# Hand-written orders for the last chunk, inverses earlier, a V split later, bias constants behind a mark

## The chip, the cores and the metric

One core of a Trainium2 chip runs the whole program. The metric is the device time of one execution in microseconds (us); the median of three runs of the kernel before is 841.37 us.

## The reference, cut to what matters

Sliding-window attention, a dense gated layer, and a routed layer of eight experts, one behind the other, all in float32 (`moe_w_*` arrive as float64 and are converted on the chip):

```python
scores = where(mask, q @ k.T / sqrt(64) + slope * -|i - j|, -1e9)     # 4 x 8 heads, 576 x 576, window 128
attn = softmax(scores) @ v
x = attn.transpose(0, 2, 1, 3).reshape(2304, 512)
x = ((x @ w_a) * (x @ w_b)) @ w_out                    # d_ff = 1536
logits = x @ w_gate + modality_bias[modality_id]       # 8 experts
e = argmax(logits); gate = softmax(logits)[e]
out[token] = gate * (relu(x @ w1[e]) @ w2[e])          # F = 1024
```

## The kernel before

The 2304 tokens are cut into seven chunks of 3, 2, 2, 3, 3, 3 and 2 tiles of 128 (`CH`, L34). A chunk goes through the dense layer in twelve steps `j`, one for each 128 columns of `d_ff`: `mm_ab` (L485) makes `x @ w_a` and `x @ w_b` in two PSUM banks (`psa`, `psb`), ScalarE copies the first out (`asb`), VectorE multiplies (`gf`), and one step later `mm_out` (L501) adds the product times `w_out` into PSUM. From chunk 1 on, `gf` is split into a rounded part (ScalarE cast) and a rest (VectorE subtraction), since matmuls run on pairs of reduced-precision values.

**Attention runs inside the steps of the chunk ahead.** One item is one 128-row tile of a pair of heads. An item takes three steps: in the first its scores are computed (`score_mm`), reduced on VectorE (`score_red`) and exponentiated on ScalarE; in the second VectorE inverts the sum (`score_invs`, two small instructions), ScalarE scales by it (`score_nrm`, L295), TensorE transposes (`pt_tr`, L304), ScalarE and VectorE copy and split (`pt_cp`, L317 and L318), and GpSimd masks it into `pt` (L320, L322); in the third TensorE multiplies by V (`a_pv`, L370) and ScalarE copies out (`pv_out`, L379). V has a split of its own (`prep_va` on ScalarE, `prep_vd` on VectorE) out of `vr`, which has a single buffer, so the next pair's load waits for it.

**Chunk 0** is special twice. Its own attention runs ahead of everything, items 0 to 11, in the first 42 us (the head). Its twelve steps (`step0`) then also convert the float64 weights on VectorE: for each step three instructions on 128x1024 words (`f64_ops`, tile `f64f`), the subtraction `rest` (L444) behind ScalarE's cast (`hi`, L441), and three on 128x512 words for `w_out` (`f64o`). I call this VectorE's list of a step: `step0` takes turns between `da` (`rest` and the three `f64f`) and `db` (the three `f64o`, then the inverses). `mm_out` of the step before waits for the third `f64o`; `late_rests` and `gf` stand behind the whole list.

**Orders.** In `step0` and `step` (chunks 1 to 5) the order on TensorE, ScalarE and VectorE is the order of the code (`tc.manual_schedule`); a planner orders SyncE's DMA queue and GpSimd, and, in chunk 6, all engines. Each engine runs its queue in order. In chunk 6 (two tiles, 256 columns) there is no attention left; it carries the routing of chunks 4 and 5: 24 dot products (`rd_dot`, L593, three for each expert, whose gate row `wgt` comes by DMA into one of two halves), then `route_fin` for three tiles, the choice of the expert that starts first (`early`), the gather of its tokens, the split of its `w1` (L877) and the transposes of its tokens (`u_xT`). The expert layers follow (L1190, L1207): `gen0` is the first.

`consts_b` builds the table of modality biases on GpSimd in six instructions (L755 to L765) from a small load `mid_i`. The code calls it in step 2 of chunk 0; the planner is free to put it earlier.

Of the kernel before, what the change touches and what calls it, by code (L numbers as in the profile page):

```python
# [7 lines left out]
F32 = mybir.dt.float32  # L8
F32R = mybir.dt.float32r
# [5 lines left out]
ALU = mybir.AluOpType  # L15
# [6 lines left out]
def attn_moe_moe2(ctx: ExitStack, tc, q, k, v, moe_w_a, moe_w_b, moe_w_out, modality_id,  # L22
# [18 lines left out]
    RD = (2, 3, 4, 5)  # L41
    PCB = 1
    LDA = 6
    EJ = 1
    SAT = 3
    PRP = 1
    HPS = 2000
# [611 lines left out]
    def new_preps(gk, gv):  # L659
        d = stage["d"]  # L660
        for a in stage["k"]:
            for h in range(2):
                prep_qa(a, h)
                d.append(lambda a=a, h=h: prep_qd(a, h))
        stage["q"] += stage["k"]
        stage["k"] = []
        while pos["prep"] < len(plist) and first[plist[pos["prep"]]] < gk:
            a = pairs[plist[pos["prep"]]]
            if a.c in S32:
                a_prep_q(a)  # L670
                prep_va(a)
                d.append(lambda a=a: prep_vd(a))
                pos["prep"] += 1
                continue
            prep_ka(a)
            d.append(lambda a=a: prep_kd(a))
            stage["k"].append(a)
            pos["prep"] += 1
        while stage["q"] and first[stage["q"][0].c, stage["q"][0].hp] < gv:
            a = stage["q"].pop(0)  # L680
            prep_va(a)
            d.append(lambda a=a: prep_vd(a))
# [191 lines left out]
    def split(dst, srcw, early=False):  # L874
# [4 lines left out]
        for k in range(srcw.shape[1]):  # L879
            nc.scalar.copy(out=dst[:, 0, k], in_=srcw[:, k])  # L880
            (nc.gpsimd if k < W2P else nc.vector).tensor_tensor(out=dst[:, 1, k], in0=srcw[:, k], in1=dst[:, 0, k], op=ALU.subtract)

    def u_w1(ev, pool):
        W1 = []
        for f in range(4):
            r = pool.tile([P, KD, 2 * P], F32, tag="wr", name="wr1")
            nc.sync.dma_start(out=r.rearrange("p k f -> p (k f)"),
                              in_=w1[bass.ds(ev, 1), f].rearrange("o p x -> p (o x)"))
            t = w1p.tile([P, 2, KD, 2 * P], F32R, tag="w1", name="w1s")
            split(t, r)  # L890
            W1.append(t)
        return W1

    def u_w2(ev, pool, early=False):
        W2 = []
# [22 lines left out]
        with tc.high_priority(offset=HPXT):  # L918
            return u_xT_(xg, nt, pool, bank)

    def u_xT_(xg, nt, pool, bank):
        xT = pool.tile([P, 2, KD, UT], F32R, tag="xT", name="xT")
        for kk in range(KD):
            ps = bank("ps_t")
            for t in range(nt):
                nc.tensor.transpose(ps[:, t * P:(t + 1) * P], xg[:, t, kk * P:(kk + 1) * P], ident)
            nc.scalar.copy(out=xT[:, 0, kk, :nt * P], in_=ps[:, :nt * P])
            nc.vector.tensor_tensor(out=xT[:, 1, kk, :nt * P], in0=ps[:, :nt * P], in1=xT[:, 0, kk, :nt * P],
                                    op=ALU.subtract)
        return xT  # L930
# [34 lines left out]
    def step0(j, pend, sc, tp):  # L965

        n, last = CH[0] * P, j == NJ - 1
        new = list(range(cur["s"], goal[j]))
        its = [live[g] for g in tp] if j else []
        if j + 2 < NJ:  # L970
            job[j + 2] = wab_jobs(j + 2)
        js = job.get(j + 2, [])

        da = [job.pop(j + 1)[4]] if j + 1 in job else []
        da += js[:3 if j else 2]
        db = [f for i in ((j - 1, j) if last else (j - 1,)) if i >= 0 for f in wo_jobs(i)]
        for g in sc:
            db += score_invs(live[g])
        while da or db:
            for d in (da, db):  # L980
                if d:
                    d.pop(0)()
        psa = mm_ab(0, j, 0, None if j else 1)
        asb = m1.tile([P, MT * P], F32, tag="asb", bufs=1, name="asb")
        nc.scalar.copy(out=asb[:, :n], in_=psa[:, :n])
        for g in sc:
            score_nrm(live[g])
        late_rests()
        psb = mm_ab(0, j, 1)
        gf = m1.tile([P, MT * P], F32, tag="g", bufs=2, name="gf")  # L990
        nc.vector.tensor_tensor(out=gf[:, :n], in0=psb[:, :n], in1=asb[:, :n], op=ALU.mult)
        for f in () if j else js[2:3]:
            f()
        for it in its:
            a_pv(it)
        for g in sc:
            pt_tr(live[g])
            pt_cp(live[g])
        z_add()
        for it in its:  # L1000
            pv_out(it)
        for g in new:
            c_, hp_, t_ = items[g]
            live[g] = score_mm(pairs[c_, hp_], t_)
        for f in js[3:4]:
            f()
        for g in new:
            score_red(live[g])
        for g in new:
            score_exp(live[g])  # L1010
        new_preps(goal[j + 2], goal[j])
        if pend is not None:
            mm_out(*pend, wo_t[j - 1])
        if last:
            wo_fetch(0, 1)
            wo_fetch(1, 1)
            x_split(1)
        cur["s"] = goal[j]
        for g in tp if j else ():
            live.pop(g)  # L1020
        return (0, j, gf), new, sc if j else tp + sc
# [77 lines left out]
    def evac(c):  # L1099
# [3 lines left out]
        now.extend(rd)  # L1103
        rd.clear()

    pe = ExitStack()
    for c in range(NC):
        n = CH[c] * P
        for j in range(NJ):
            if c == 0:  # L1110
                if j == 0:
                    sc, tp = [n0 + 1], [n0]
                    pe.enter_context(tc.manual_schedule(engines={
                        mybir.EngineType.PE, mybir.EngineType.Activation, mybir.EngineType.DVE}))
                if j + 4 < NJ:
                    wab_load(j + 4)
                if j:
                    wo_load(j)
                if j == CJ:
                    consts_b()  # L1120
                a_loads(goal[j] + LDA)
                pend, sc, tp = step0(j, pend, sc, tp)
                continue
            if j == 0:
                if c == NC - 1:
                    assert not sc and not tp and cur["s"] == len(items)
                    pe.close()
                if c - 1 in RD:
                    rd_fetch(0)
                    rd_fetch(1)  # L1130
                mm_out(*pend, *([wo_t[NJ - 1]] if c == 1 else []))
                pend = None
                if c in (1, NC - 1):
                    evac(c - 1)
            if c > 1:
                wo_fetch(j, c)
            if c < NC - 1:
                a_loads(goal[c * NJ + j] + LDA)
                if c == 3 and (j == 5 or j > 5 and zr):
                    x2_init()  # L1140
                pend, sc, tp = step(c, j, pend, sc, tp)
                continue
            if j == EJ:
                at_st.close()
                w1p = ctx.enter_context(tc.tile_pool(name="w1p", bufs=4, side="right"))
                wrp = ctx.enter_context(tc.tile_pool(name="wrp", bufs=1, side="right"))
                xgp = ctx.enter_context(tc.tile_pool(name="xgp", bufs=1, side="right"))
                early()
                e0v = ld(uv0, 0, E - 1)
                g0 = u_gather(ld(uv0, 1, (E - 1) * RG), 3, xgp)  # L1150
                W1 = u_w1(e0v, wrp)
            if j == EJ + 4:
                xT0 = u_xT(g0[1], 3, xgp, at_bank)
            psa = mm_ab(c, j, 0)
            asb = m1.tile([P, MT * P], F32, tag="asb", bufs=1, name="asb")
            nc.scalar.copy(out=asb[:, :n], in_=psa[:, :n])  # L1156
            psb = mm_ab(c, j, 1)
            gf = m1.tile([P, MT * P], F32, tag="gf", bufs=1, name="gf")
            nc.vector.tensor_tensor(out=gf[:, :n], in0=psb[:, :n], in1=asb[:, :n], op=ALU.mult)
            gt = m1.tile([P, 2, MT * P], F32R, tag="g", bufs=2, name="g")  # L1160
            nc.scalar.copy(out=gt[:, 0, :n], in_=gf[:, :n])
            nc.vector.tensor_tensor(out=gt[:, 1, :n], in0=gf[:, :n], in1=gt[:, 0, :n], op=ALU.subtract)
            if j > 0:
                mm_out(*pend)
            pend = (c, j, gt, wo_t[j])
            if now and j < E // 2:
                rd_dot(2 * j)
                rd_dot(2 * j + 1)
                if j == E // 2 - 1:
                    rd_fin()  # L1170
                    for r in ranks:
                        for _ in r[1]:
                            pass
                    ranks.clear()
    wab_st.close()
    w2p = ctx.enter_context(tc.tile_pool(name="w2p", bufs=4))
    wrq = ctx.enter_context(tc.tile_pool(name="wrq", bufs=4))
# [34 lines left out]
                                           op0=ALU.max, op1=ALU.subtract)  # L1212
        yield from u_gemm2(h, W2, xg, idx, 3, bank, fo)

    gen0 = u_big(*g0, xT0, W1, u_w2(e0v, wrq, W2E), at_bank, FO0)

    def adv(n):
        for _ in range(n):
# [235 lines left out]
```

## Time and profile before

| | |
|---|---|
| median of 3 runs | 841.37 us (841.33 to 843.8) |
| the profiled execution, its span | 844.7 us, 843.0 us |
| TensorE matmul busy | 805.0 us, 95% of the span |
| VectorE, ScalarE, GpSimd busy | 65%, 55%, 27% |
| mean granted TensorE clock | 0.987 of 2.4 GHz |

Busy time is that of one profiled execution. TensorE's matmuls are pipelined and their ends are modelled, so what matters is not its share but the idle time ahead of an instruction, the instruction that released it, and the granted clock. A row of the timeline is: start, duration, engine, line and operation, out<-in, tile and shapes, count, and in brackets the idle time before it and what ended that. The clock has two levels, 1.2 and 2.4 GHz; a stretch's mean says how much of it ran at the lower one.

### The profile page before, as it was taken

How to read it: one execution, taken by the hardware profiler on the slowest of the kernel's cores; microseconds unless marked ns; L12 is line 12 of the kernel's file. 1: busy time of each engine (PE TensorE's matmuls, PEld its weight loads, DVE VectorE, ACT ScalarE, POOL GpSimd, SP SyncE). 2: the span in 40 equal slices, each digit the busy share in tenths (PEclk: the TensorE clock that was granted, in tenths of full speed). 3: DMA queues.
4: the chain of work that ended last, by engine and by line, in shares of the span. 5: the costliest groups of instructions: out<-in, count | busy, mean ns of one | idle time of the engine just before them, and what ended most of it. 6: DMA issues, size and time to landing. Idle time of an engine off the chain costs nothing.

```text
span 843.0 us, 14389 instructions
## 1 busy us (share of the span) xinstructions
PE 805.0 (95%) x4686; PEld 724.9 (86%) x4686; DVE 544.5 (65%) x1571; ACT 461.3 (55%) x1161; POOL 230.7 (27%) x365
## 2 busy tenths in 40 slices
PE   8887999999999999999999999998999999999994
PEld 6764777899899999999999999997988998989793
DVE  7777978677667676667777776377376544447420
ACT  6843444877878876666667644233245443547420
POOL 5432121243233432232223331120133030114101
PEclk9998999999999999999999999999999999999998
DMA  8992325667656695554555543476428564549301
GB/s 245 381 357 94 118 94 156 182 219 230 206 157 181 184 227 160 155 150 139 162 154 153 126 152 120 131 224 221 108 88 302 204 193 134 166 137 304 109 26 40
DMA packets 78629, 145.13 MB, mean 172 GB/s; under 512 B 14095, under 2 KB 41903, under 8 KB 78544
## 3 DMA queue, kind: packets, MB, share of 16 engines
q1 hardware_dynamic: 74992, 134.39, 52.7%
q0 software_dynamic: 3552, 9.73, 3.3%
q8 instruction: 39, 0.64, 0.3%
q14 instruction: 46, 0.38, 0.1%
HBM read 118.16 MB, written 22.12 MB: 166 GB/s over the span
## 4 chain that ended last, share of the span: by engine, by line
PE 63%; DVE 10%; issue 8%; DMA 8%; ACT 7%; POOL 1%; SPq 1%; POOLq 0%; ACTq 0%; DVEq 0%
PE ps_ab L494 26%; PE acc L511 11%; PE ps_h L1207 7%; PE ps_y L1190 7%; PE ps_o L370 2%; PE ps_s L252 2%; DVE f64f L418 2%; PE ps_p L304 2%; PE acc L507 2%; DMA vr<-in_v 2%; DMA wr<-in_moe_w 1%; DMA wraw<-in_moe_w_b 1%; ACT p L276 1%; DMA wgt<-in_wgt 1%; DVE f64o L418 1%
## 5 line engine op out<-in xcount | busy, mean ns | idle before, releaser
L494 PE MATMUL ps_ab<-xr,wab 128*128 128x384 f32 (+1 forms) x2016 | 328.0, 318 | 3.5 <-ACT asb L1156 1.7
L494 PEld LDWEIGHTS ps_ab<-xr,wab 128*128 128x128 f32 x2016 | 309.2, 190 | 15.7 <-issue 4.4
L511 PE MATMUL acc<-wo,g 128*128 128x512 f32 x540 | 135.8, 393 | 0.0
L320 POOL TENSOR_SCALAR_AFFINE_SELECT pt<-pc 128x512 fp32r<-128x512 f32 (+1 forms) x72 | 46.0, 638 | 283.5 <-DVE pc L318 263.9
L511 PEld LDWEIGHTS acc<-wo,g 128*128 128x128 f32 x540 | 96.8, 188 | 16.5
L1207 PE MATMUL ps_h<-xT,w1s 128*128 128x384 f32 x576 | 104.3, 338 | 0.0
L1190 PE MATMUL ps_y<-w2s,h 128*128 128x512 f32 x432 | 104.0, 395 | 0.0
L1207 PEld LDWEIGHTS ps_h<-xT,w1s 128*128 128x128 f32 x576 | 99.7, 188 | 1.3 <-issue 0.5
L1190 PEld LDWEIGHTS ps_y<-w2s,h 128*128 128x128 f32 x432 | 79.8, 188 | 15.7
L276 ACT ACTIVATE p<-p,mx 128x128 f32<-128x128 f32 x144 | 56.7, 395 | 28.9 <-DVE mx L266 28.7
L593 DVE CUSTOM_DVE_ANT_0 junk<-x,wgt 128x512 f32<-128x512 f32 x88 | 62.1, 706 | 6.2 <-DMA wgt<-in_wgt 4.2
L295 ACT ACTIVATE p<-p,mx 128x128 f32<-128x128 f32 x120 | 41.7, 395 | 41.3 <-DVE mx L284 41.2
L379 ACT COPY u<-ps_o 64x384 f32<-64x384 f32 x120 | 56.8, 473 | 7.8 <-PE ps_o L370 6.3
L1062 ACT CAST g<-gf 128x384 fp32r<-128x384 f32 (+1 forms) x60 | 28.2, 471 | 50.6 <-DVE gf L1060 50.1
L1063 DVE TENSOR_TENSOR g<-gf,g 128x384 fp32r<-128x384 f32 (+1 forms) x60 | 30.6, 510 | 37.7 <-ACT g L1062 37.7
L877 DVE TENSOR_TENSOR w2s<-wr,w2s 128x1024 fp32r<-128x1024 f32 x24 | 29.4, 1225 | 39.3 <-ACT w2s L876 39.2
L1197 POOL DMA_INDIRECT out<-y,idx x18 | 21.2, 1176 | 114.1 <-ACT y L1196 112.6
L1060 DVE TENSOR_TENSOR gf<-ps_ab,asb 128x384 f32<-128x384 f32 (+1 forms) x60 | 30.1, 502 | 32.6 <-PE ps_ab L494 25.5
L322 POOL TENSOR_SCALAR_AFFINE_SELECT pt<-pc 128x512 fp32r<-128x512 f32 (+1 forms) x72 | 47.1, 654 | 0.0
L1210 ACT ACTIVATE h<-ps_h 128x384 fp32r<-128x384 f32 x48 | 23.5, 492 | 42.8 <-PE ps_h L1207 42.8
L304 PE MATMUL ps_p<-ident,p 128*128 128x128 f32 x144 | 31.5, 288 | 13.9 <-ACT p L295 12.5
L877 DVE TENSOR_TENSOR w1s<-wr,w1s 128x1024 fp32r<-128x1024 f32 x28 | 34.3, 1224 | 16.1 <-ACT w1s L876 15.9
(216 smaller groups left out, 1203.8 us busy)
## 6 DMA issues: line engine op xcount, KB each, us to landing
wo<-wo_d SPq DMA_DIRECT2D x60, 512.0 KB, 3.9
wr<-in_moe_w SPq DMA_DIRECT2D x56, 512.0 KB, 4.3
wgt<-in_wgt SPq DMA_DIRECT2D x32, 256.0 KB, 3.7
wraw<-in_moe_w_a SPq DMA_DIRECT2D x12, 512.0 KB, 8.4
wraw<-in_moe_w_b SPq DMA_DIRECT2D x12, 512.0 KB, 9.0
wor<-in_moe_w_out SPq DMA_DIRECT2D x12, 512.0 KB, 3.6
wo_d<-wo SPq DMA_DIRECT2D x12, 512.0 KB, 3.1
kr<-in_k SPq DMA_DIRECT2D x24, 256.0 KB, 4.2
```

The lines of the kernel that those rows point to most:

```text
L276: nc.scalar.activation(out=it.p[:, h, :], in_=it.p[:, h, :], func=AF.Exp, bias=it.mx[:, 2 + h:3 + h], scale=-1.0, accum_out=it.mx[:, 4 + h ...
L295: nc.scalar.activation(out=it.p[:, h, :], in_=it.p[:, h, :], func=AF.Copy, scale=it.mx[:, 6 + h:7 + h])
L304: nc.tensor.transpose(it.pp[:, h, :], it.p[:, h, :], ident)
L320: nc.gpsimd.affine_select(out=it.pt[:, :, 0], in_=pc, pattern=pat + [[-1, P]], base=0, channel_multiplier=1, compare_op=ALU.is_gt, fill=0.0)
L322: mark["pt"] = nc.gpsimd.affine_select(out=it.pt[:, :, 1], in_=pc, pattern=pat + [[1, P]], base=0, channel_multiplier=-1, compare_op=ALU.i ...
L379: nc.scalar.copy(out=u[o:o + 64], in_=it.po[o:o + 64, 1 - h:4 - h])
L494: nc.tensor.matmul(ps[:, :n], lhsT=w[:, m, r, kk * P:(kk + 1) * P], rhs=xr[:, s, kk, :n], start=(idx == 0), stop=(idx == len(terms) - 1))
L511: nc.tensor.matmul(acc[c, t], lhsT=g[:, r, t * P:(t + 1) * P], rhs=w[:, s, :], start=(j == 0 and idx == 0), stop=(j == NJ - 1 and idx == 2))
L593: nc.vector.tensor_tensor_reduce(out=junk, in0=x2[:, 0:DM], in1=wgt[0][:, e % 2], scale=1.0, scalar=0.0, op0=ALU.mult, op1=ALU.add, accum_ ...
L877: nc.vector.tensor_tensor(out=dst[:, 1], in0=srcw, in1=dst[:, 0], op=ALU.subtract)
L1190: nc.tensor.matmul(pss[t], lhsT=h[:, r, f, t * P:(t + 1) * P], rhs=W2[f // 2][:, s_, f % 2, :], start=(f == 0 and i == 0), stop=(f == 7 an ...
L1207: nc.tensor.matmul(ps, lhsT=W1[f // 2][:, r, kk, (f % 2) * P:(f % 2 + 1) * P], rhs=xT[:, s_, kk, :], start=(kk == 0 and i == 0), stop=(kk ...
```

## The change

Four edits:

1. Chunk 0's list: `db` is now the first inverse instruction, the first `f64o`, the second inverse instruction, the other `f64o`.
2. A chunk 1 pair's V split no longer stands where its Q is prepared but is queued (`stage["q"]`), and comes in the first step whose scores need that pair: for the pairs prepared in steps 0, 2 and 4 that is step 1, 4 and 6.
3. `consts_b` may be issued only behind the last `pt` mask traced by then.
4. Chunk 6 gets a function `step6`; its three compute engines follow the code. One expert's dots per step (steps 0 to 7) in place of two (0 to 3); `early`, the gather and the first `w1` load in step 0 in place of 1; `w1` splits in steps 3, 5, 7, 9; transposes in 5 and 6; routing of chunk 5 in steps 8 to 11.

```diff
@@ step0
-        db = [f for i in ((j - 1, j) if last else (j - 1,)) if i >= 0 for f in wo_jobs(i)]
-        for g in sc:
-            db += score_invs(live[g])
+        di = [f for g in sc for f in score_invs(live[g])]
+        dw = [f for i in ((j - 1, j) if last else (j - 1,)) if i >= 0 for f in wo_jobs(i)]
+        db = di[:1] + dw[:1] + di[1:] + dw[1:]
@@ new_preps
             if a.c in S32:
                 a_prep_q(a)
-                prep_va(a)
-                d.append(lambda a=a: prep_vd(a))
+                stage["q"].append(a)
@@ chunk 0's loop
                 if j == CJ:
-                    consts_b()
+                    with tc.issue_after(mark["pt"]):
+                        consts_b()
@@ chunk 6
+    def step6(j, pend):
+        psa = mm_ab(c, j, 0)
+        nc.scalar.copy(out=asb[:, :n], in_=psa[:, :n])
+        if j == 0:
+            evac(c - 1)
+        for _ in range(2 if j == NJ - 1 else 1):
+            if ranks and ranks[0][0] == 2:
+                next(ranks.pop(0)[1], None)
+        for r in ranks:
+            if r[0] < 2:
+                next(r[1])
+                r[0] += 1
+        psb = mm_ab(c, j, 1)
+        nc.vector.tensor_tensor(out=gf[:, :n], in0=psb[:, :n], in1=asb[:, :n], op=ALU.mult)
+        nc.scalar.copy(out=gt[:, 0, :n], in_=gf[:, :n])
+        nc.vector.tensor_tensor(out=gt[:, 1, :n], in0=gf[:, :n], in1=gt[:, 0, :n], op=ALU.subtract)
+        if j == 0:
+            early()
+            un0["e"] = ld(uv0, 0, E - 1)
+            un0["g"] = u_gather(ld(uv0, 1, (E - 1) * RG), 3, xgp)
+            un0["r"], un0["w"] = w1_load(un0["e"], wrp, 0), []
+        if j in (5, 6):
+            un0["x"] = u_xT_(un0["g"][1], 3, xgp, at_bank, range(2 * (j - 5), 2 * (j - 5) + 2), un0.get("x"))
+        if j in (3, 5, 7, 9):
+            un0["w"].append(w1_split(un0["r"]))
+            if j < 9:
+                un0["r"] = w1_load(un0["e"], wrp, len(un0["w"]))
+        if now:
+            rd_dot(j)
+            if j == E - 1:
+                rd_fin()
+        if pend is not None:
+            mm_out(*pend)
```

## Rows read from the trace of the kernel before

**Rows 1.** Stretches: length, TensorE, its weight loads, VectorE, ScalarE, GpSimd, clock, DMA, GB/s
```profile
20.00:40.00 20.00, 17.54 (x112) 14.97 (x111) 14.86 (x58) 17.24 (x69) 10.18 (x23) 0.92 1.01 368
...
60.00:80.00 20.00, 13.78 (x61) 10.93 (x60) 16.21 (x27) 7.90 (x21) 3.09 (x7) 0.91 0.33 107
80.00:100.00 20.00, 19.03 (x78) 14.01 (x79) 15.81 (x30) 9.42 (x20) 3.36 (x7) 0.91 0.35 111
...
560.00:580.00 20.00, 17.08 (x109) 15.33 (x109) 14.35 (x38) 4.95 (x11) 4.25 (x4) 0.91 0.80 258
```

**Rows 2.** TensorE's waits over the whole span: total us, times, longest
```profile
PE ps_p L304 <- ACT p L295: 12.5, 9, 4.4
PE ps_o L336 <- POOL pt L320: 1.9, 2, 1.3
```

**Rows 3.** Timeline of GpSimd in the head
```profile
17.35 0.20 POOL L755 CAST mid<-mid_i 128x18 f32<-128x18 int32 x1 [3.39 <-DMA mid_i<-in_moe_modality_id]
...
18.85 1.39 POOL L761 TENSOR_TENSOR bm<-tb,mb 128x144 f32<-128x144 f32 x1
```

**Rows 4.** Timeline of ScalarE, step 1 of chunk 0
```profile
57.37 0.51 ACT L198 CAST vv<-vr 128x384 fp32r<-128x384 f32 x1 [5.26 <-DMA vr<-in_v]
```

**Rows 5.** Timeline of TensorE, the transposes of steps 2, 3, 5, 7 and 9 of chunk 0
```profile
67.68 0.77 PE L304 MATMUL ps_p<-ident,p 128*128 128x128 f32 x2 [4.44 <-ACT p L295]
...
79.58 0.62 PE L304 MATMUL ps_p<-ident,p 128*128 128x128 f32 x2 [1.78 <-ACT p L295]
...
97.74 0.62 PE L304 MATMUL ps_p<-ident,p 128*128 128x128 f32 x2 [0.97 <-ACT p L295]
...
116.75 0.62 PE L304 MATMUL ps_p<-ident,p 128*128 128x128 f32 x2 [0.89 <-ACT p L295]
...
133.78 0.62 PE L304 MATMUL ps_p<-ident,p 128*128 128x128 f32 x2 [1.58 <-ACT p L295]
```

**Rows 6.** Timeline of VectorE: the `rest` of steps 2 and 3; the list of step 5
```profile
61.22 1.23 DVE L444 TENSOR_TENSOR wab<-f64f,wab 128x1024 fp32r<-128x1024 f32 x1 [1.39 <-ACT wab L441]
...
71.09 2.97 DVE L444 TENSOR_TENSOR wab<-f64f,wab 128x1024 fp32r<-128x1024 f32 x1
...
91.28 1.22 DVE L444 TENSOR_TENSOR wab<-f64f,wab 128x1024 fp32r<-128x1024 f32 x1 [0.23 <-ACT wab L441]
...
95.10 0.69 DVE L418 SCALAR_TENSOR_TENSOR f64o<-wor,f64o 128x512 uint32<-128x512 uint32 x1
95.70 1.22 DVE L418 SCALAR_TENSOR_TENSOR f64f<-wraw,f64f 128x1024 uint32<-128x1024 uint32 x1
...
97.03 0.17 DVE L284 RECIPROCAL mx<-mx 128x2 f32<-128x2 f32 x1
```

**Rows 7.** Timeline of TensorE: into chunk 6, two of its steps, and the first expert
```profile
549.68 1.64 PE L511 MATMUL acc<-wo,g 128*128 128x512 f32 x6
...
581.12 2.98 PE L494 MATMUL ps_ab<-xr,wab 128*128 128x256 f32 x24
...
585.33 2.98 PE L494 MATMUL ps_ab<-xr,wab 128*128 128x256 f32 x24
...
609.59 2.79 PE L1207 MATMUL ps_h<-xT,w1s 128*128 128x384 f32 x15
```

**Rows 8.** Timeline of VectorE: a dot of chunk 5; the first and last of 21 routing instructions
```profile
480.45 0.69 DVE L593 CUSTOM_DVE_ANT_0 junk<-x,wgt 128x512 f32<-128x512 f32 x1
...
530.16 0.16 DVE L538 TENSOR_TENSOR lg<-lgr,bm 128x8 f32<-128x8 f32 x1
...
533.34 0.23 DVE L557 TENSOR_SCALAR oh<-iot,sc 128x8 bf16<-128x8 f32 x1
```

**Rows 9.** Timeline of VectorE: the subtraction behind `gf` in a step of chunk 6
```profile
589.24 0.42 DVE L1162 TENSOR_TENSOR g<-gf,g 128x256 fp32r<-128x256 f32 x1 [0.47 <-ACT g L1161]
```

**Rows 10.** The page: the groups of `w1` splits, then gate-row loads (KB each, us to landing)
```profile
L877 DVE TENSOR_TENSOR w1s<-wr,w1s 128x1024 fp32r<-128x1024 f32 x28 | 34.3, 1224 | 16.1 <-ACT w1s L876 15.9
...
wgt<-in_wgt SPq DMA_DIRECT2D x32, 256.0 KB, 3.7
```

More of the change, by code (lines that the diff above doesn't have):

```diff
@@ L43, in attn_moe_moe2 @@
     LDA = 6
-    EJ = 1
     SAT = 3
@@ L881, in split, with w1_load, w1_split @@
             (nc.gpsimd if k < W2P else nc.vector).tensor_tensor(out=dst[:, 1, k], in0=srcw[:, k], in1=dst[:, 0, k], op=ALU.subtract)
-    def u_w1(ev, pool):
[L884 to L892, printed above, removed]
+    def w1_load(ev, pool, f):
+        r = pool.tile([P, KD, 2 * P], F32, tag="wr", name="wr1")
+        nc.sync.dma_start(out=r.rearrange("p k f -> p (k f)"), in_=w1[bass.ds(ev, 1), f].rearrange("o p x -> p (o x)"))
+        return r
+    def w1_split(r):
+        t = w1p.tile([P, 2, KD, 2 * P], F32R, tag="w1", name="w1s")
+        split(t, r)
+        return t
+    def u_w1(ev, pool):
+        return [w1_split(w1_load(ev, pool, f)) for f in range(4)]
     def u_w2(ev, pool, early=False):
@@ L919, in u_xT, with u_xT_ @@
             return u_xT_(xg, nt, pool, bank)
-    def u_xT_(xg, nt, pool, bank):
-        xT = pool.tile([P, 2, KD, UT], F32R, tag="xT", name="xT")
-        for kk in range(KD):
+    def u_xT_(xg, nt, pool, bank, kks=range(KD), xT=None):
+        if xT is None:
+            xT = pool.tile([P, 2, KD, UT], F32R, tag="xT", name="xT")
+        for kk in kks:
             ps = bank("ps_t")
@@ L1104, in evac @@
         rd.clear()
+    un0 = {}
+    def step6(j, pend):
+        c, n = NC - 1, CH[NC - 1] * P
+        psa = mm_ab(c, j, 0)
+        asb = m1.tile([P, MT * P], F32, tag="asb", bufs=1, name="asb")
+        nc.scalar.copy(out=asb[:, :n], in_=psa[:, :n])
[9 more added lines that the diff above has]
+        psb = mm_ab(c, j, 1)
+        gf = m1.tile([P, MT * P], F32, tag="gf", bufs=1, name="gf")
+        nc.vector.tensor_tensor(out=gf[:, :n], in0=psb[:, :n], in1=asb[:, :n], op=ALU.mult)
+        gt = m1.tile([P, 2, MT * P], F32R, tag="g", bufs=2, name="g")
+        nc.scalar.copy(out=gt[:, 0, :n], in_=gf[:, :n])
[17 more added lines that the diff above has]
+            mm_out(*pend)
+        return c, j, gt, wo_t[j]
     pe = ExitStack()
@@ L1126, in attn_moe_moe2 @@
                     assert not sc and not tp and cur["s"] == len(items)
-                    pe.close()
+                    at_st.close()
+                    w1p = ctx.enter_context(tc.tile_pool(name="w1p", bufs=4, side="right"))
+                    wrp = ctx.enter_context(tc.tile_pool(name="wrp", bufs=1, side="right"))
+                    xgp = ctx.enter_context(tc.tile_pool(name="xgp", bufs=1, side="right"))
                 if c - 1 in RD:
@@ L1132, in attn_moe_moe2 @@
                 pend = None
-                if c in (1, NC - 1):
+                if c == 1:
                     evac(c - 1)
@@ L1142, in attn_moe_moe2 @@
                 continue
[L1143 to L1174, printed above, removed]
+            pend = step6(j, pend)
+    assert not ranks and not tr and not now
+    pe.close()
     wab_st.close()
@@ L1213, in u_big @@
         yield from u_gemm2(h, W2, xg, idx, 3, bank, fo)
-    gen0 = u_big(*g0, xT0, W1, u_w2(e0v, wrq, W2E), at_bank, FO0)
+    gen0 = u_big(*un0["g"], un0["x"], un0["w"], u_w2(un0["e"], wrq, W2E), at_bank, FO0)
     def adv(n):
```

## The prediction

> **What bounds the kernel now.** I read the stretches first: TensorE is the engine that is hardly ever idle, so time can only be won where it stands still or runs at the lower clock. Up to its last stretch that is the head, chunk 0's loop and one place in chunk 6; four such stretches stand in [rows 1]. Then TensorE's waits: 12.5 us in nine waits of a transpose for `score_nrm`, and 1.9 us for a GpSimd mask [rows 2]. Then, at each of these places, the timelines of all engines. The reader is to see that in chunk 0 the transpose waits for ScalarE, which waits for an inverse that ended VectorE's list: in step 5 the list runs from 91.28 to the reciprocal at 97.03 to 97.20, and the transpose starts at 97.74 [rows 5, 6]. From chunk 1 to 5 nothing stands still, so what chunk 0 gives back should reach the end. Two steps of chunk 6 lie 4.21 us apart; I use that below as its pace [rows 7].
>
> **Edit 1, the inverses.** Nothing is added. Behind the reciprocal now stand one `f64f` and two `f64o` instructions that stood ahead of it. By the starts 95.10, 95.70 and 97.03 (the first inverse instruction 0.2 ahead of that, at 96.83) one `f64o` takes 0.60 and one `f64f` 1.13, so the reciprocal comes 2.33 us sooner in its list [rows 6]. Waits below that go to nothing: 1.78 in step 3, 1.58 in step 9, and three in steps 5 to 7, the first 0.97 and the last 0.89, 2.6 together [rows 5]. What is late next is the third `f64o`, now last in the list, for which `mm_out` waits. In step 5 it would end where the list ended, at 97.2; TensorE was free from 96.77 (97.74 less its wait), has a transpose and a score to do, some 1.2 us (an estimate), and gets to `mm_out` at about 97.9: no wait. In step 9, with no score between, I count 0.6 of the 1.58 as lost again. `gf` and `late_rests` stay behind the whole list, at the same time. So edit 1 gives 1.8 + 2.6 + 1.0 = 5.4 us outside step 2.
>
> **Edit 2, the V split.** In step 0 ScalarE stood 5.26 us in front of a V that came at 57.37, and `asb` of step 1 and the next cast `hi` stood behind it [rows 4]. A step later the V has landed. TensorE itself gains next to nothing in step 1 (0.3, an estimate), for its `mm_out` waits there for the first `f64o`s, which nothing moves. But the list of step 2, which started at 61.22 after a wait for `hi` [rows 6], starts about 2.2 earlier, where VectorE ends what it has to do in step 1. With edit 1's 2.33 that covers the 4.44 us wait of step 2 [rows 5]. On SyncE the next V load is issued a step or two later, since the single `vr` is freed later; it is needed three to four steps on. ScalarE and VectorE do the same work elsewhere, where each has room.
>
> Waits removed in the loop: 5.4 + 4.4 = 9.8, and 0.3 in step 1. Two stretches of 20 us ran at a mean clock of 0.91 right behind the longest waits [rows 1]: 1.8 us each if TensorE had work all the time, 0 if the dips stay. I take 2.5 of the 3.6, since the waits ahead of them nearly vanish.
>
> **Edit 3, the bias table.** In the head GpSimd stood 3.39 us in front of `mid_i`'s load, with a mask queued behind it, and then held a second mask for a two-input instruction of 1.39 us [rows 3]. TensorE's own wait for a mask was at most 1.3 [rows 2], but ScalarE, the fullest engine of the head (17.24 of 20 us, rows 1), stood too, and it paces the rest. At least 1.3, at most 3.4; I take 2.5, because both delays lie on the mask's path. `consts_b` now runs behind the masks of step 0, in a stretch where GpSimd has little to do (3.09 of 20 us a little later, rows 1) and nobody awaits it.
>
> Its new neighbour is VectorE's list of step 1. A `rest` beside GpSimd's masks and memsets took 2.97 us in place of 1.22 [rows 6]: 1.75 for one meeting. Bounds: 0, if GpSimd gives way, and 3.0, its own busy time before; I take 1.0, nearer to the one meeting seen. By the Trainium skill (SBUF — State Buffer, section "Who interferes with whom") a VectorE instruction with two SBUF inputs and a GpSimd instruction that reads SBUF exclude each other for the whole of the one that came first. By that rule each of the six table instructions could hold the list once, 3.0 in all, and the sum would be 2.0 later. The 2.97 row agrees with it.
>
> Head and loop: 2.5 + 9.8 + 0.3 + 2.5 - 1.0 = 14.1 us less.
>
> **Edit 4, chunk 6.** From chunk 5's last `mm_out` at 549.68 to the first expert at 609.59 are 59.9 us [rows 7]. Twelve steps at 4.21 are 50.5, that `mm_out` 2.1 (nine matmuls; six took 1.64 with their tail); 7.3 us are over: 2.9 idle, about 1.8 of clock (20 x 0.09) [rows 1], and 2.6 of transposes and small matmuls, which stay. Does the new order lose less? TensorE's next `psb` needs `gf`, and VectorE does in order, for each step: `gf` to the end of the subtraction 1.3, with 0.47 of waiting for ScalarE inside [rows 9], and three dots at 0.73, 2.2 [rows 8]: 3.5 in steps 0 to 7. Added: `early` 1.7 (nine small ones at 0.18, an estimate from 3.4 us for 21, rows 8), routing 0.9 in step 1 and 3.4 in step 8, three `w1` splits of 1.2 [rows 10] with 0.6 of waiting for ScalarE's cast, four transposes' splits, 2.0. From the end of `psb` in step 0 to `gf` of step 8: 28 + 1.7 + 0.9 + 3.4 + 5.4 + 2.0 + 0.4 = 41.8. TensorE wants that `gf` for `psb` of step 9, after 9 x 4.21 - 1.4 + 1.1 of transposes = 37.6. So it stands some 4.2 us: about 1 in step 2, the rest in step 9 behind the routing instructions. With 0.3 at the end and 0 to 1.8 of clock behind the long stall, chunk 6 takes 59.7 to 61.5 against 59.9; I take 0.7 more. Below: 4.5 less, if VectorE keeps up; above: 3 more. The first `w1` and the gather come a step sooner and are needed three and five steps later; SyncE stands for the expert's number until `early` is done, with gate rows behind it that are needed two steps on.
>
> **The sum.** 844.7 - 14.1 + 0.7 = 831.3. The profiled execution is 3.3 us above the median shown (844.7 against 841.37), so I predict 828.0, with 824 to 832 as this case's own range (head, clock and meetings each at either bound in part).
>
> **Rivals.**
> - *VectorE takes the wait's place* (0.20). Its list of 5.9 us [rows 6] and the product, split, V and score reduction behind it (some 2.4, an estimate) come to 8.3 us, about what TensorE has to do in a step, and neither gets shorter. If freed waits come back at `mm_out` (3 of 9.8), the clock dips stay (0), one meeting costs 1.75 and the head gives 1.3, the gain is 6.8 + 0.3 - 1.75 + 1.3 - 0.7 = 6.0: 835.4. For it: 16.21 of 20 busy [rows 1]. Against: much of the rest is waiting for TensorE.
> - *VectorE keeps up in chunk 6* (0.09): the routing overlaps or packs closer, no stall, 5 us less: 823.
> - *The V load holds SyncE* (0.07): it waits for the later split ahead of a `w_out` load, whose conversion heads the next list. Two pairs at up to 6 us each eat 12 of 14: 840, no change. Against: every `w_out` load has about a step to spare.
> - *Gate rows pace chunk 6* (0.06), slower. A row half is fetched when its last dot is done and is needed two steps later. With a pace of 4.9 for VectorE (41.8 less `early` and a part of step 8's routing, over eight steps) that leaves 2 x 4.9 - 2.2 = 7.6 us; they landed in 3.7 [rows 10]. The queue is in order and also holds `w1` and `w_out` loads that wait for others. If each of the six fetches comes later than 7.6, all of VectorE's queue waits, `gf` too; from 2.6 us late each (10.2 in all) it costs 16 and eats the whole gain: 844 and more.
>
> **Chances.** The forecast 0.58, the others as given. About 0.3%, 2.5 us, is what a measurement of this kernel tells from no change. Faster: 0.58 + 0.20 + 0.09 = 0.87; same 0.07; slower 0.06. The range 822 to 837 holds the forecast, the second rival and most of the first; 0.13 and the first one's tail stay out.
>
> **What would show it.** In chunk 0: transposes with waits under 0.5, steps of about 8.3 us, `asb` of step 1 at about 50 rather than behind 57.37, and chunk 1 starting about 14 us sooner. In the head: no GpSimd wait for `mid_i`. In chunk 6: TensorE waiting for `gf`, about 1 us in step 2 and 3 to 4 in step 9, behind 21 routing instructions. I am wrong if `mm_out` waits for `f64o` in most steps, if a dot waits for its gate row, or if chunk 6 changes by over 4 us.

## The result

The changed kernel took **829.6 us** (median of 4 runs, 828.85 to 830.77), the kernel before 842.59 in the same series: ratio 0.9846, interval 0.9822 to 0.9871, so 13.0 us less. Run again later beside two variants it took 831.08 (ratio 0.9879, 0.9857 to 0.9901; 10.2 us less). The prediction was 828.0, with 822 to 837 as its range. The profiled execution took 828.85 us, its span 827.1, 15.9 us less than that of before; these two executions are the slowest of the one kernel and the fastest of the other in that series, so 15.9 and not 13.0.

Where the 15.9 us went can be read from one row of each step: ScalarE's copy `asb`, which comes when the first matmuls of the step have ended. Its starts, in us:

| | step 0 | step 1 | step 3 | chunk 1 | chunk 5 | end |
|---|---|---|---|---|---|---|
| before | 43.11 | 57.79 | 75.35 | 156.30 | 471.64 | 842.97 |
| after | 40.02 | 49.05 | 67.07 | 141.54 | 456.65 | 827.13 |
| sooner by | 3.09 | 8.74 | 8.28 | 14.76 | 14.99 | 15.84 |

The head gives 3.1, chunk 0's loop 11.7, chunks 1 to 4 pass it on, and chunks 5 and 6 with the experts add 0.85. These are single executions: edit 4 alone, further down, leaves chunk 0 as it was, and its profile reaches chunk 1 at 154.51, not 156.30; a second profile of the changed kernel reaches it at 142.44. Between these four profiles chunk 1 comes 12.1 to 14.8 us sooner. First the stretches of the changed kernel that answer to [rows 1], with the one behind them:

```profile
20.00:40.00 20.00, 17.49 (x117) 15.03 (x117) 15.63 (x62) 16.66 (x66) 8.57 (x20) 1.00 1.00 367
60.00:80.00 20.00, 18.37 (x85) 14.08 (x84) 19.03 (x32) 8.71 (x20) 7.88 (x11) 1.00 0.50 158
80.00:100.00 20.00, 20.00 (x93) 15.69 (x92) 19.51 (x42) 10.68 (x29) 4.31 (x7) 1.00 0.37 107
560.00:580.00 20.00, 17.23 (x124) 16.00 (x124) 16.84 (x56) 7.15 (x20) 0.00 (x0) 1.00 0.68 209
580.00:600.00 20.00, 19.75 (x124) 18.22 (x124) 9.86 (x32) 8.06 (x18) 5.63 (x5) 0.91 0.41 146
```

From 60 to 100 TensorE is busy for 38.4 us of 40, where it was for 32.8, and its clock is 1.00 where it was 0.91. VectorE is now as full as TensorE (38.5 of 40). In chunk 6 the 0.91 has moved one stretch on, behind a stall. TensorE's waits over the whole span, which answer to [rows 2], the longest three:

```profile
PE acc L506 <- DVE f64o L417: 4.7, 5, 2.0
PE ps_ab L493 <- DVE gf L1126: 3.0, 2, 2.8
PE ps_p L303 <- ACT p L294: 2.1, 3, 1.5
```

The transposes' 12.5 us are 2.1, and of these 1.46 stand in step 0, where they stood before. The GpSimd mask's 1.3 is gone. What came in their place is an output matmul that waits for the third `f64o`, four times, 0.48 to 1.11 us (the first row, 1.98 us in step 1, stood there before with 1.74):

```profile
53.40 2.84 PE L506 MATMUL acc<-f64o,gf 128*128 128x512 f32 x6 [1.98 <-DVE f64o L417]
...
62.04 2.84 PE L506 MATMUL acc<-f64o,gf 128*128 128x512 f32 x6 [0.52 <-DVE f64o L417]
...
71.02 2.84 PE L506 MATMUL acc<-f64o,gf 128*128 128x512 f32 x6 [1.11 <-DVE f64o L417]
...
103.59 2.84 PE L506 MATMUL acc<-f64o,gf 128*128 128x512 f32 x6 [0.57 <-DVE f64o L417]
...
119.37 2.84 PE L506 MATMUL acc<-f64o,gf 128*128 128x512 f32 x6 [0.48 <-DVE f64o L417]
```

ScalarE in step 1 answers to [rows 4]. `asb` runs at 49.05, the V comes as late as ever (57.5), and what stood 5.26 us in front of it now stands 0.75:

```profile
49.05 0.48 ACT L986 COPY asb<-ps_ab 128x384 f32<-128x384 f32 x1
...
57.52 0.52 ACT L197 CAST vv<-vr 128x384 fp32r<-128x384 f32 x1 [0.75 <-DMA vr<-in_v]
58.41 0.48 ACT L986 COPY asb<-ps_ab 128x384 f32<-128x384 f32 x1 [0.38 <-PE ps_ab L493]
```

The bias table now runs in step 1 on GpSimd, beside VectorE's list (engines POOL and DVE in turn):

```profile
50.31 1.16 POOL L757 TENSOR_SCALAR tb<-mid 128x18 f32<-128x18 f32 x2
50.69 0.68 DVE L417 SCALAR_TENSOR_TENSOR f64o<-wor,f64o 128x512 uint32<-128x512 uint32 x1
51.29 1.21 DVE L417 SCALAR_TENSOR_TENSOR f64f<-wraw,f64f 128x1024 uint32<-128x1024 uint32 x1
51.44 1.35 POOL L759 TENSOR_TENSOR bm<-tb,mb 128x144 f32<-128x144 f32 x1
52.43 0.92 DVE L417 SCALAR_TENSOR_TENSOR f64o<-wor,f64o 128x512 uint32<-128x512 uint32 x1
52.76 0.88 POOL L761 TENSOR_TENSOR tb<-tb,mb 128x144 f32<-128x144 f32 x1
53.27 1.45 DVE L417 SCALAR_TENSOR_TENSOR f64f<-wraw,f64f 128x1024 uint32<-128x1024 uint32 x1
53.71 1.35 POOL L763 TENSOR_TENSOR bm<-bm,tb 128x144 f32<-128x144 f32 x1
```

One `f64o` took 0.92 where its neighbour took 0.68, and one `f64f` 1.45 where the one ahead took 1.21 (the same four durations stand in the profile of edit 3 alone); the table's six instructions took 5.1 us in sum (the load's cast, 0.38, is not shown). In chunk 6, VectorE's routing (21 instructions, first and last shown), the product behind it, and TensorE, which waits for that product:

```profile
576.24 0.16 DVE L537 TENSOR_TENSOR lg<-lgr,bm 128x8 f32<-128x8 f32 x1
...
579.09 0.23 DVE L556 TENSOR_SCALAR oh<-iot,sc 128x8 bf16<-128x8 f32 x1
...
579.23 0.42 DVE L1126 TENSOR_TENSOR gf<-ps_ab,asb 128x256 f32<-128x256 f32 x1
...
579.70 2.29 PE L493 MATMUL ps_ab<-xr,wab 128*128 128x256 f32 x12 [2.77 <-DVE gf L1126]
```

### The profile page after: what moved, and what is told of

Same layout as the page of the kernel before. It is cut to its first block, busy times and chain, and to the rows that moved or that the text cites. A ratio compares the mean times of both kernels' runs of the same rounds, so it can differ in the third digit from the quotient of the medians.

```text
span 827.1 us, 14384 instructions
## 1 busy us (share of the span) xinstructions
PE 798.5 (97%) x4686; PEld 722.1 (87%) x4686; DVE 547.4 (66%) x1571; ACT 461.3 (56%) x1161; POOL 235.3 (28%) x365
## 4 chain that ended last, share of the span: by engine, by line
PE 61%; DVE 13%; issue 9%; ACT 7%; DMA 5%; POOL 2%; SPq 2%; POOLq 0%; ACTq 0%; DVEq 0%
PE ps_ab L493 24%; PE acc L510 10%; PE ps_h L1225 8%; PE ps_y L1208 8%; PE acc L506 3%; PE ps_o L369 2%; PE ps_s L251 2%; DVE f64f L417 1%; ACT p L275 1%; DVE junk L592 1%; DMA wraw<-in_moe_w_a 1%; PE ps_p L303 1%; DVE p L265 1%; ACT g L1063 1%; DMA kk<-in_k 1%
## 5 line engine op out<-in xcount | busy, mean ns | idle before, releaser
L319 POOL TENSOR_SCALAR_AFFINE_SELECT pt<-pc 128x512 fp32r<-128x512 f32 (+1 forms) x72 | 47.2, 656 | 263.2 <-DVE pc L317 240.6
L321 POOL TENSOR_SCALAR_AFFINE_SELECT pt<-pc 128x512 fp32r<-128x512 f32 (+1 forms) x72 | 48.2, 669 | 0.0
L1229 DVE SCALAR_TENSOR_TENSOR h<-ps_h,h 128x384 fp32r<-128x384 f32 x48 | 26.3, 554 | 27.8 <-ACT h L1228 27.6
```

Of the source, the lines that this page charges most:

```text
L319: nc.gpsimd.affine_select(out=it.pt[:, :, 0], in_=pc, pattern=pat + [[-1, P]], base=0, channel_multiplier=1, compare_op=ALU.is_gt, fill=0.0)
L321: mark["pt"] = nc.gpsimd.affine_select(out=it.pt[:, :, 1], in_=pc, pattern=pat + [[1, P]], base=0, channel_multiplier=-1, compare_op=ALU.i ...
```

## The experiments

First each edit alone, the pairs, and the first three together; then two moves on top of the changed kernel. "Change" is the ratio to the kernel before, run on the same chip, less 1, times its median. The columns behind it are the starts of `asb` in one profiled execution of each.

| kernel | median | before | change, 95% interval (us) | `asb` step 0 / 1 / 3 | chunk 1 |
|---|---|---|---|---|---|
| edit 1 | 832.72 | 842.34 | -10.1 (-12.4 to -7.7) | 47.80 / 57.71 / 77.04 | 151.44 |
| edit 2 | 839.27 | 842.34 | -2.8 (-4.5 to -1.1) | 44.98 / 54.02 / 73.69 | 152.52 |
| edit 3 | 841.17 | 842.34 | -1.5 (-2.6 to -0.3) | 42.46 / 57.93 / 75.76 | 154.27 |
| edits 1, 2 | 834.81 | 842.34 | -7.7 (-9.8 to -5.6) | 45.26 / 54.28 / 73.43 | 147.94 |
| edits 1, 3 | 832.38 | 840.55 | -9.0 (-10.8 to -7.1) | 42.45 / 58.00 / 72.52 | 146.40 |
| edits 2, 3 | 835.74 | 841.37 | -5.8 (-7.2 to -4.5) | 42.33 / 51.36 / 71.57 | 150.44 |
| edits 1, 2, 3 | 829.48 | 841.34 | -11.6 (-13.7 to -9.6) | 41.31 / 50.34 / 68.35 | 142.82 |
| edit 4 | 843.09 | 841.34 | +2.0 (0.6 to 3.4) | 45.62 / 57.27 / 74.52 | 154.51 |
| changed kernel again | 831.08 | 840.55 | -10.2 (-12.0 to -8.3) | 39.97 / 49.01 / 67.89 | 142.44 |
| routing moved | 828.75 | 841.34 | -12.5 (-14.5 to -10.5) | 42.43 / 51.47 / 70.08 | 144.58 |
| `f64o` moved | 828.19 | 841.34 | -13.5 (-15.5 to -11.4) | 41.08 / 50.11 / 67.32 | 140.32 |
| both moved | 824.80 | 840.55 | -15.4 (-17.8 to -13.0) | 41.04 / 50.08 / 67.29 | 140.31 |

**Edit 1 alone**: the inverses early (`step0` of the change), all else as before.

> The kernel before with edit 1 alone (the inverses early in VectorE's list, the V split where it was). Theory A, the prediction's: the inverses were what the transposes waited for, so the waits outside step 2 (5.4 us) go, the 4.44 in step 2 shrinks by the 2.33 that the reciprocal comes sooner, and one of the two clock dips partly goes (about 1): 7.5 to 9 us faster. Rival B, the late V set the pace: the list of step 2 still starts late, and what is won in steps 3 to 9 comes back at the output matmuls, which wait for the last f64o: 4 us faster at most, both dips stay.

Measured: 10.1 us less, 1.1 beyond theory A's range and well beyond B's. The transposes' waits are gone, that of step 2 too; but a clock dip stays (0.83 from 60 to 80 us), as B has it. The profiled execution took 837.63 us at a mean clock of 0.983, the other four 830.76 to 835.79 at 0.991 to 0.994. From step 3 to chunk 1 the loop took 74.4 us. In the seven kernels with edit 1 and without the later `f64o` move it took 73.9 to 74.6 there, on average 74.4, in the five without edit 1 (the kernel before among them) 78.5 to 81.0, on average 79.4: **edit 1 is worth 5.0 us from step 3 on**, the clearest number of the study, since both groups lie apart. The transposes' waits of 5.3 to 6.7 us in that stretch are gone, and 1.7 to 2.2 us of waits for `f64o` stand there in their place; about 1 us of TensorE's busy time went too (73.3 and more against 72.2 to 72.4).

**Edit 2 alone**: V split a step later (`new_preps` of the change).

> The kernel before with edit 2 alone (chunk 1's V split a step later, the inverses last as before). Theory A: the list of step 2 starts some 2.2 us sooner and its wait of 4.44 falls to about 2.2; the later steps keep their waits; with some clock 2 to 4 us faster. Rival B, the late V set the pace: the wait of step 2 goes nearly whole and the stretch behind it runs at full clock: 5 to 8 us faster. Rival C, the later split holds SyncE: no gain or slower.

Measured: 2.8 us less, as theory A has it. `asb` of step 1 comes at 54.02 and no longer behind the V. The wait of step 2 is not halved but gone, which is rival B's half of it; the transposes of the other steps still wait, 7.2 us in sum. Step 3 comes only 1.7 us sooner, since the head of this execution was 1.9 us later than that of before (44.98 against 43.11). Nothing shows that the later split holds SyncE (rival C).

**Edits 1 and 2 together.**

> Edits 1 and 2 together, the bias table and chunk 6 as before. Theory A: the loop gives all that it gives in the changed kernel, 10 to 12.6 us, a little more than the sum of the two alone, since only both cover the 4.44 of step 2 and both clock dips go. Rival: the parts overlap, and together they give less than the sum by 2 us or more.

Measured: 7.7 us less; theory A (10 to 12.6) fell. The two alone add up to 12.9. In the head the bias table still stands on GpSimd, and in this execution TensorE waits 2.83 us for the mask behind it (GpSimd's row, then TensorE's):

```profile
17.67 0.20 POOL L754 CAST mid<-mid_i 128x18 f32<-128x18 int32 x1 [4.07 <-DMA mid_i<-in_moe_modality_id]
...
19.76 1.97 PE L336 MATMUL ps_o<-raw,pt 128*128 128x64 f32 x8 [2.83 <-POOL pt L320]
```

Step 3 comes at 73.43, hardly sooner than with edit 2 alone. That this pair came out no better than edit 1 alone is within the intervals of both, and by the estimate at the end of this section most of it is clock.

**Edit 3 alone**: the bias table behind the masks of step 0.

> The kernel before with edit 3 alone (the bias table behind the masks of step 0). The changed kernel's trace has its first ab matmul 3.1 us sooner, and step 1 0.25 longer. Theory A: that is the bias table alone and reaches the end: 2.3 to 3.5 us faster. Rival: with the long list of step 1 ahead of the transposes the table's meeting with VectorE costs more here, where nothing else is relieved (1.0 and up), or ScalarE's wait for V eats the head's gain, because the V lands when it lands: 0 to 1.5 us faster.

Measured: 1.5 us less, where the head alone would have given 3.1. The rival is right in its second form. The head is faster, but ScalarE then stands 6.05 us in front of a V that lands at 57.51, and `asb` of step 1 is at 57.93, as before. In all five kernels that split V in step 0 the cast stands between 56.85 and 57.58, while their `asb` of step 0 stands anywhere from 42.45 to 47.80. So the V lands at a time of its own. That is theory P of the next runs.

**Edits 1 to 3, chunk 6 as before.**

> Edits 1 to 3 together, chunk 6 as before; the changed kernel without edit 4. In the kernel with edit 3 alone the cast of V still ended where the V landed, near 57.5 us, so the head's gain was lost there. Theory P (the landing of V pins step 1 as long as its split stands in step 0): with edit 2 beside it edit 3 is worth its whole 3 us and keeps the clock up in the head, so this kernel is 12 to 14.5 us faster than before, like the changed kernel. Rival: edit 3 is worth the same 1.2 us here as alone, so this one is 9 to 10.5 us faster, and edit 4 must have given the rest.

Measured: 11.6 us less, 0.4 short of P's range and 1.1 beyond the rival's. Added to edits 1 and 2, edit 3 gave 3.9, and alone 1.5. Step 3 is at 68.35 in place of 73.43, with the head 4.0 us sooner: P, by the trace.

**Edits 1 and 3**: edit 2 left out.

> Edits 1 and 3, V split where it was, chunk 6 as before; it is set against edits 1 to 3 together (11.9 us faster than before) and edit 1 alone (10.1). Theory P, the landing of V near 57.5 us pins step 1: the head's gain of 3 us is lost there, so 9 to 10.5 us faster, with asb of step 1 near 57.8 in the trace. Rival: the place of V's split is worth nothing beside edits 1 and 3: 11.5 to 12.5 us faster.

Measured: 9.0 us less, at P's edge, and `asb` of step 1 at 58.00, behind this row of ScalarE:

```profile
57.58 0.51 ACT L198 CAST vv<-vr 128x384 fp32r<-128x384 f32 x1 [6.12 <-DMA vr<-in_v]
58.00 0.47 ACT L985 COPY asb<-ps_ab 128x384 f32<-128x384 f32 x1
```

**Edits 2 and 3**: the inverses last as before.

> Edits 2 and 3 together, the inverses last as before, chunk 6 as before. Alone they gave 2.8 us (edit 2) and 1.5 (edit 3), 4.3 in sum. Theory P, the V that lands near 57.4 us pins step 1 as long as its split stands in step 0, and the bias table holds up the head as long as it stands there: only both together let step 3 begin sooner, so they give more than their sum, 6 to 9 us, with asb of step 3 at 68 to 71 us in the trace (75.35 before, 73.69 with edit 2 alone, 75.76 with edit 3 alone). Rival: they add, 3.5 to 5 us.

Measured: 5.8 us less, between the two expectations (the sum of the parts is 4.3), step 3 at 71.57, just outside P's 68 to 71. So P's direction holds and its size was too large for this pair. Over all four contexts edit 3 gave, without edit 2, 1.5 and -1.1, and with edit 2 3.0 and 3.9: worth nothing certain without it, some 3.4 with it (each of these differences has the spread of two intervals behind it).

**Edit 4 alone**: `step6` of the change in the kernel before.

> The kernel before with edit 4 alone (the written order of chunk 6; chunk 0 as before). Theory A, the prediction's: VectorE's queue is full for eight steps, the stall in front of the product behind the routing costs what the written order saves: 0.7 us slower, between 1.5 faster and 2 slower, with a wait of TensorE for gf of 2.5 to 4 us in step 9. Rival: the stall is paid for by time saved elsewhere in the chunk and in the first expert's start, so alone it is 2 us or more faster.

Measured: 2.0 us more, at theory A's upper edge; the rival fell. TensorE stands 3.1 us for `gf` in step 9, up to 592.8; the clock of the 20 us that hold this stall is 0.91 (and that of the 20 us behind it too), while it is 1.00 ahead of them:

```profile
560.00:580.00 20.00, 20.00 (x144) 18.72 (x143) 16.23 (x43) 5.69 (x12) 3.87 (x4) 1.00 0.85 281
580.00:600.00 20.00, 16.93 (x114) 15.80 (x113) 14.73 (x58) 6.66 (x18) 0.00 (x0) 0.91 0.50 171
```

**The changed kernel again**, as the neighbour of the last variants.

> The changed kernel as it is, beside the two others on the same chip: 12 to 13.5 us faster than before.

Measured: 10.2 us less, below the expectation, though the first series gave 13.0; the intervals overlap (10.9 to 12.0). The stretch behind the stall shows part of it: its clock is 0.83 here, not 0.91.

```profile
580.00:600.00 20.00, 19.04 (x110) 17.48 (x111) 8.35 (x33) 6.15 (x14) 4.16 (x4) 0.83 0.36 116
```

**Routing behind the product**, in every step of chunk 6, on top of the changed kernel.

```diff
-        for _ in range(2 if j == NJ - 1 else 1):
-            ...
-        for r in ranks:
-            ...
         psb = mm_ab(c, j, 1)
         ...
         nc.vector.tensor_tensor(out=gt[:, 1, :n], in0=gf[:, :n], in1=gt[:, 0, :n], op=ALU.subtract)
+        for _ in range(2 if j == NJ - 1 else 1):
+            ...
+        for r in ranks:
+            ...
```

> The changed kernel with one move in chunk 6: the routing instructions of a step go behind that step's product and split, where they stood ahead of the product. Theory A: the 2.77 us for which TensorE stood in step 9 are those instructions (3.1 us of VectorE), and the 0.91 clock of the stretch behind is a consequence of the stall: the stall goes and the clock stays at 1.00: 2.5 to 4 us faster than the changed kernel, 15.5 to 17 faster than before. Rival: VectorE's queue is full whatever the order, the stall moves one step on: within 1 us of the changed kernel.

Measured: 12.5 us less, within 1 us of the changed kernel's first median (829.6, on another chip), as the rival has it, but not for the rival's reason. The 2.77 us stall is gone and the clock is 1.00. Three other waits came: 1.49 for the routing that `early` needs in step 0, 0.93 for `asb`, which stands on ScalarE behind the routing's exponentials, and 1.48 in the last step:

```profile
544.12 0.17 PE L938 MATMUL ps_n<-osum,ones 128*128 128x8 bf16 x1 [1.49 <-DVE osum L567]
...
584.61 3.11 PE L493 MATMUL ps_ab<-xr,wab 128*128 128x256 f32 x24 [0.93 <-ACT asb L1114]
...
593.61 0.17 PE L566 MATMUL ps_r<-osum,ones 128*128 128x8 bf16 x1 [1.48 <-DVE osum L567]
```

Two of the three come from steps in which nothing had to be moved.

**The third `f64f` behind the `f64o`**, on top of the changed kernel.

```diff
+        q = []
         while da or db:
             for d in (da, db):
                 if d:
-                    d.pop(0)()
+                    q.append(d.pop(0))
+        if j and js:
+            q.remove(js[2])
+            q.append(js[2])
+        for f in q:
+            f()
```

> The changed kernel with one move in chunk 0's loop: from step 1 on the third f64f goes behind the f64o instructions, so that the output matmul's f64o ends 1.23 us sooner in the list and the f64f for the next step's cast ends last. Theory A: the waits of the output matmuls (1.98 in step 1 and four of 0.48 to 1.11) go, the cast still ends ahead of the next list: 1.5 to 3.5 us faster than the changed kernel, 14.5 to 16.5 faster than before. Rival: VectorE's work of a step, some 8.1 us, is what paces the loop, so the wait only changes its place (the next rest, or the next product): within 1 us of the changed kernel.

Measured: 13.5 us less, 1 us short of theory A's range. The trace favours theory A: of the five waits for `f64o` only that of step 1 is left (1.97), a transpose waits 0.51 in their place, and from step 2 to chunk 1 the loop is 1.5 to 2.3 us shorter (80.9 against 82.4 and 83.1 in the two profiles of the changed kernel, `asb` to `asb`). The medians, 828.19 against 829.6 and 831.08, agree in sign, but they are from different chips and their intervals overlap, so the times alone do not show it.

**Both moves**, the routing's only in step 8, where the stall was.

```diff
         for r in ranks:
-            if r[0] < 2:
+            if r[0] < 2 and j != E:
                 next(r[1])
                 r[0] += 1
         ...
         nc.vector.tensor_tensor(out=gt[:, 1, :n], in0=gf[:, :n], in1=gt[:, 0, :n], op=ALU.subtract)
+        if j == E:
+            for r in ranks:
+                next(r[1])
+                r[0] += 1
```

(and the diff of the `f64o` move.)

> The changed kernel with two moves: in chunk 0's loop the third f64f behind the f64o instructions, and in step 8 of chunk 6, there alone, the first part of the routing behind the product and the split. Theory A: the two gains add: in the trace 2.3 us of the loop and of the 2.77 us stall all but the 0.9 for which asb then waits behind the routing's ScalarE instructions, with the clock that stays up: 3 to 5 us faster than the changed kernel of the same call. Rival: within 1 us of it, since VectorE's work paces both places.

Measured: **824.8 us, 6.3 less than the changed kernel on the same chip**, and 15.4 less than the kernel before; its five runs (823.78 to 829.2) all lie below the four of the changed kernel (830.87 to 831.83). That is more than theory A asked for. From the start of `asb` in step 0 of chunk 6 to step 11 it takes 48.55 us, where the changed kernel took 53.22 on this chip and 51.95 in its first profile. Part of that is clock, which was 0.83 behind the stall in the one and 0.91 in the other (3.4 and 1.8 us of 20). Of the stall 0.99 is left, and the clock stays up:

```profile
579.65 1.69 PE L493 MATMUL ps_ab<-xr,wab 128*128 128x256 f32 x12 [0.99 <-ACT asb L1120]
```

```profile
560.00:580.00 20.00, 19.01 (x135) 17.41 (x134) 16.65 (x60) 7.61 (x20) 0.00 (x0) 1.00 0.62 193
580.00:600.00 20.00, 19.22 (x132) 17.88 (x131) 12.61 (x30) 10.07 (x20) 8.62 (x7) 1.00 0.41 146
```

**The same runs at equal clock.** Each execution's mean granted clock is on record, and its time multiplied by that clock is a rough estimate of its time at 2.4 GHz throughout: rough, since it treats an execution as if TensorE's clock paced all of it, and since the lower clock often stands right behind a wait and may belong to the kernel. Averaged over the executions of a kernel and set against the kernel before on the same chip, it gives 6.7 us less for edit 1, 1.7 for edit 2, 0.2 for edit 3; 7.5 for edits 1 and 2, 6.8 for 1 and 3, 5.3 for 2 and 3, 10.1 for all three; and 0.1 for edit 4, each good to about 1 us. By this estimate some 3 us of edit 1's 10.1 are clock, and edits 1 and 2 nearly add (7.5 against 8.4). Edits 2 and 3 together still give far more than their sum (5.3 against 1.9), so clock does not explain the interplay that theory P names. The 2.0 us that edit 4 costs would be clock altogether.

## Why the prediction was right, and where its terms were off

**The time** came out at 829.6 against 828.0, inside the range. The prediction's gain was 13.4 us; the first series gave 13.0, the second 10.2. Head and loop were to give 14.1; chunk 1 starts 12.1 to 14.8 sooner. Several terms were off in ways that cancelled, so that the sum came so near is in part luck.

**Edit 1.** Right in mechanism and near in size: 5.4 predicted outside step 2, 5.0 measured from step 3 on. The step that failed is "no wait" at the output matmul in step 5 and 0.6 lost in step 9. `mm_out` took back 2.7 us in steps 2, 3, 7 and 9 (1.98 in step 1 is 0.24 more than before). In step 5 itself there is indeed no wait, and waits in five steps of twelve are fewer than the "most steps" that were to show the prediction wrong. The error was to carry its 0.7 us of margin over to the other steps: from 60 to 100 us VectorE is busy for 38.5 of 40, so it has little to spare. This is the rival "VectorE takes the wait's place", in part: it had said 3 of 9.8. It didn't win, because its other parts (dips that stay, a small gain in the head) did not come true. The 4.44 us of step 2, by the prediction, took both edits to cover. But nothing of it is left in the profiles of edit 1 alone and of edit 2 alone, and with edit 4 alone, where chunk 0 is unchanged, it is 2.52 (with edits 1 and 3, 1.22). So its size was in part that one execution's.

**Edit 2** was right for what it does (`asb` "at about 50": 49.05), wrong in being priced by itself. With the V landing at 57 us whatever comes ahead, the gain in the head could only pass through if the V no longer stood in the way of step 1. The sum held because both edits were there; by the prediction's terms edit 3 alone should have given its 2.5 less 1.0 and did (1.5), but for another reason: the head's gain ended at the V.

**The clock.** 2.5 of 3.6 taken, and all 3.6 came: 1.00 in both stretches, in every profile with edits 1 to 3. But that the dips followed these waits is not shown. Edit 4 alone kept 10.9 us of the transposes' waits and ran at 1.00 in both stretches, and edit 1 alone lost them and ran at 0.83 from 60 to 80.

**Edit 3, the head.** 2.5 predicted, 3.1 found, both from the one trace of before. Over more traces it is larger: the first wait for `qq` ends at 33.20 to 35.70 in the five kernels whose table stands in the head, and at 29.75 to 30.12 in the nine profiles where it doesn't: 3.1 to 6.0 apart. Not all of that is waiting: from 20 to 30 us the mean clock was 0.68 to 0.84 in those five and 1.00 in the nine, which can be 1.6 to 3.2 us of the difference (10 us times what is missing to 1.00). From 30 to 40 it is the other way round (1.00 in the five, 0.73 to 0.83 in seven of the nine), so at `asb` of step 0 the groups lie only 0.7 to 7.8 apart. The bound of 3.4 was one draw of a load's landing: GpSimd stood 3.39 there [rows 3], and 3.63 to 4.08 in the other four.

**The meeting with VectorE** was over-priced: 1.0 taken, and 0.48 of lengthening is seen in the two instructions of the list. Whether any of it reached TensorE is not shown: its wait for `f64o` in step 1 is 1.97 to 1.98 us in every kernel whose table stands there, and 1.74 to 2.25 in the others. It was mostly GpSimd that gave way: its six instructions took 5.12 us, and 2.1 to 3.0 where they stood in the head. The step that failed was to size the term by a meeting in which VectorE was the one that waits. By the Trainium skill (SBUF — State Buffer, section "Who interferes with whom") the one that issues first keeps the shared ports for its whole instruction and the other waits. The trace agrees: `bm` at 51.44 started 0.15 behind an `f64f` and ended 0.29 behind its end, and the `f64o` at 52.43, which started ahead of the end of that `bm`, took 0.24 more.

**Edit 4.** The stall came where it was put, behind the 21 routing instructions in step 9, with 2.77 in place of some 3.2, and 0.22 in step 2 in place of 1. The net of +0.7 was to lie between -4.5 and +3. From the end of chunk 5's last `mm_out` to the first expert the profile of after gives 57.95. That of before gives 57.33, or 58.27 from the six of its nine matmuls that ran ahead of chunk 6's first two: so +0.6 or -0.3. Edit 4 alone gave +2.0. From chunk 5 to the end, the four traces with edit 4 as it is take 371.2 us on average and the eight without it 370.1: +1.1, with overlap (370.5 to 372.5 against 368.7 to 371.4). It cost about what was said, a good part of it as clock behind the stall, which was 0.83 to 0.95 in all four; the bound of 1.8 for that was too low where it was 0.83 (20 x 0.17 = 3.4). Of the two rivals in chunk 6, gate rows cost next to nothing (one dot waited for its row, 0.45 us, though that was to be a sign of being wrong), and VectorE did not keep up.

**The V load on SyncE** held nothing up that the profiles show: in none of the kernels with edit 2 do they list a wait of VectorE for a load in chunk 0.

## What to carry to other kernels

An engine's queue has an order within one step too: put what another engine waits for ahead of what is only needed a step later, which was worth 5 us here for two small instructions, and some 5 to 6 more when done at two further places. Two delays in a row (a slow head, a load that lands when it lands) hide each other, so price edits together, or test them in pairs. When a wait is removed, look at the engine whose queue is then the fullest: the next wait is for the last instruction of its list.

## What was not expected of the hardware

A stall of some 3 us on TensorE cost 1 to 3.4 us more in clock: in the four profiles with the stall of step 9 the 20 us behind it ran at 0.83 to 0.95, and at 1.00 in the two variants without it. The same kernel had 0.91 there in one execution and 0.83 in another, with no row that tells them apart. Step 1 of chunk 0 shows the same with a shorter wait. In twelve profiles TensorE stands there 1.97 to 2.25 us for `f64o`; behind it the six output matmuls take 2.84 us in four of them, as in the changed kernel's row at 53.40, and 4.10 to 5.49 in eight, as here with edit 1 alone:

```profile
61.19 5.49 PE L507 MATMUL acc<-f64o,gf 128*128 128x512 f32 x6 [1.99 <-DVE f64o L418]
```

So a wait of 2 us can cost up to 2.6 us more or nothing, and such draws are as large as some of the differences between the kernels here. And where the bias table met VectorE's list, the engine with the small instructions lost more: GpSimd took 5.12 us in place of 2.1 to 3.0, VectorE's list 0.5 more.
